# A second phase in which outputs are copied one tile later, two products share a PSUM buffer, and ACT takes one more chunk of the high part

## The chip, the cores and the metric

One core of a Trainium2 chip runs the program. The metric is the device time of one execution in microseconds (us), as the median of several runs. PE is the matrix engine (TensorE), DVE the vector engine, ACT the scalar engine, POOL is GpSimd, and SP only issues transfers (DMAs). PSUM is the memory that PE writes its products to; ACT and DVE read it, POOL and DMAs don't.

## The reference

```python
X = np.fft.rfft(x, axis=1)                    # 8 x 3072 x 256, in time
Y = X @ (w_r + 1j * w_i) + (b_r + 1j * b_i)   # then shrunk by 0.01
x = np.fft.irfft(shrink(Y), axis=1).reshape(24576, 256)
c, slot_out = soft_mixture(x, phi, w1, w2)    # 24576 x 32 and 32 x 256
x = c @ slot_out
h = x @ w_in                                  # 24576 x 1024
e = np.exp(h - h.max(-1, keepdims=True))
sm = e / (e.sum(-1, keepdims=True) + 1e-9)
solu = h * sm
mu, var = solu.mean(-1), solu.var(-1)         # kept as columns
ln = (solu - mu) / np.sqrt(var + 1e-6) * g_ln
out = ln @ w_out                              # 24576 x 256
```

The layers up to `c` are the program's first phase. In the second, `h` is computed as `c` times the small matrix `slot_out @ w_in`, and the rest of the last layer follows tile by tile.

## The kernel before, in words

The second phase (`phase2`, from line 840) is a loop over 192 tiles of 128 tokens, NI tiles in groups of four (NG = 48). Nothing schedules it but the order in which the loop writes its calls: each engine takes its own instructions in that order, and semaphores make it wait for other engines. One pass i of the loop (line 1170) works on several tiles at once, each at another stage:

- `hmat(i + 3)`: PE makes the rows of h (negated) in a PSUM buffer `hps` of two banks, one of three.
- `rowmax(i + 2)`: DVE takes the row minimum (L990) into the group's small tile `st`.
- `umul(i + 1)`: DVE multiplies `hps` by `e` into `u` and sums each row (L1005).
- `blocks(i + 1)`: DVE transposes u in blocks of 32 into `tb` (L1021), and SP issues four DMAs (L1025) that put the blocks in place in `t2`, one of three buffers. The profile calls this tile `t`.
- `store(i - 4)` and `late_c`: SP issues a group's output store (L1133), or loads `ct` for later tiles.
- `outp(i - 4)`: ACT copies the finished product from PSUM to `osb`, with the row's factor as its scale (L1122). The four copies of a group fill one `osb` buffer.
- `vari(i)`: ACT sums the squares of u's distance from its mean (`sq`, L1081).
- `uhi(i - 1)`: the high part of the transposed tile, rounded to the matrix engine's fast format; of eight chunks of 128 columns ACT makes the first HA = 5 (L1061), POOL the other three (L1062).
- `ulo(i - 1, 0)` and `ulo(i - 1, 1)`: POOL subtracts the high part from the tile, in two pieces (`ul`, L1071).
- `rstd(i)`, between those two pieces: in the last pass of each group POOL computes the factor of all four tiles, five operations on 4 columns (L1104 to L1108), the last a power of -1/2 into `st`. The last group does so for each tile.
- `expo(i + 2)`: ACT takes the exponential (`e`, L997).
- `prod(i - 2)`: PE multiplies the high and low parts by the two parts of the output weights, 24 matmuls into the PSUM buffer `po2` (`po` in the profile), one of two. A product waits for the copy of the tile two before it, which had its buffer.

On ACT the order of a pass is thus: `osb` of tile i-4, `sq` of i, `uh` of i-1, `e` of i+2. The last two tiles of all are transposed on PE (`direct`) instead of by DVE and DMA.

Of the kernel before, what the change touches and what calls it, by code (L numbers as in the profile page):

```python
# [8 lines left out]
F32 = mybir.dt.float32  # L9
# [5 lines left out]
ALU = mybir.AluOpType  # L15
# [20 lines left out]
def kernel(  # L36
# [24 lines left out]
    PE, ACT, DVE, POOL, SP = nc.tensor, nc.scalar, nc.vector, nc.gpsimd, nc.sync  # L61
    B, N, D = x.shape
# [5 lines left out]
    DFF = 1024  # L68
    NI = T // 128
# [18 lines left out]
    def mm(out, lhsT, rhs, start=True, stop=True):  # L88
        PE.matmul(out=out, lhsT=lhsT, rhs=rhs, start=start, stop=stop)  # L89
# [749 lines left out]
    def phase2(p2: ExitStack, pw: ExitStack):  # L839
# [24 lines left out]
        ps = pt.tile([128, 2, 32], F32, name="pslt", tag="pt")  # L864
# [81 lines left out]
        def right(name, bufs, **k):  # L946
            return p2.enter_context(tc.tile_pool(name=name, bufs=bufs, side="right", **k))
# [7 lines left out]
        po_p = right("po_p", 2, space=PSUM)  # L955
        NG = NI // 4
        ctt, hps, et, ut, uht, stt, osb, pot = {}, {}, {}, {}, {}, {}, {}, {}
# [13 lines left out]
        def hmat(i):  # L971
            if i >= NI:
                return
            j, k = divmod(i, 4)
            ps = ph_p.tile([128, DFF], F32, name="hps", tag="hps")
            for fh in range(2):
                mm(ps[:, 512 * fh:512 * fh + 512], ctt[j][:, 128 * k:128 * k + 128], (gstn if direct(i) else gst)[:, 512 * fh:512 * fh + 512])
            hps[i] = ps
# [7 lines left out]
        def rowmax(i):  # L986
            if i >= NI:
                return
            st, k = stats(i)
            DVE.tensor_reduce(out=st[:, 0, k:k + 1], in_=hps[i], op=ALU.min, axis=AX.X)  # L990
# [9 lines left out]
        def umul(i):  # L1000
            if i >= NI:
                return
            st, k = stats(i)
            u = u_p.tile([128, DFF], F32, name="u", tag="u")
            DVE.scalar_tensor_tensor(out=u, in0=hps.pop(i), scalar=1.0, in1=et.pop(i), op0=ALU.mult, op1=ALU.mult, accum_out=st[:, 2, k:k + 1])  # L1005
            ut[i] = u
# [10 lines left out]
        def blocks(i):  # L1017
            if i >= NI or direct(i):
                return
            t = u_p.tile([128, DFF], F32, name="tb", tag="tb", bufs=3)  # L1020
            DVE.transpose(out=t, in_=ut[i])  # L1021
            t2 = u_p.tile([128, 4, 256], F32, name="t2", tag="t2", bufs=3)
            for a in range(4):
                z = slice(32 * a, 32 * a + 32)
                SP.dma_start(out=t2[:, a, :], in_=t[z].rearrange("i (b x) -> i b x", b=4))  # L1025
            t2t[i] = t2

        def trans(i):
            if i >= NI or not direct(i):
                return  # L1030
            ps = ph_p.tile([128, 8, 128], F32, name="pu", tag="hps")
            for c in range(8):
                tp(ps[:, c, :], ut[i][:, 128 * c:128 * c + 128])
            ut[i, 0] = ps
# [7 lines left out]
        def direct_parts(i):  # L1042
            if i >= NI or not direct(i):
                return
            uh, ul = parts(i)
            ps = ut.pop((i, 0))
            for n in range(2):
                z = slice(4 * n, 4 * n + 4)
                ACT.activation(out=uh[:, z, :], in_=ps[:, z, :], func=AF.Copy)
                DVE.tensor_tensor(out=ul[:, z, :], in0=ps[:, z, :], in1=uh[:, z, :].bitcast(F32), op=ALU.subtract)  # L1050


        HA = 5

        def uhi(i):
            if i < 0 or direct(i):
                return
            uh, ul = parts(i)
            v = t2t[i].rearrange("p a (c j) -> p c a j", c=8)
            w = uh.rearrange("p c (a j) -> p c a j", a=4)  # L1060
            ACT.activation(out=w[:, 0:HA], in_=v[:, 0:HA], func=AF.Copy)  # L1061
            POOL.tensor_copy(out=w[:, HA:8], in_=v[:, HA:8])  # L1062

# [12 lines left out]
        def vari(i):  # L1076
            if i >= NI:
                return
            st, k = stats(i)
            sq = e_p.tile([128, DFF], F32, name="sq", tag="sq", bufs=1)  # L1080
            ACT.activation(out=sq, in_=ut.pop(i), func=AF.Square, bias=st[:, 2, k:k + 1], scale=-float(DFF), accum_out=st[:, 3, k:k + 1])  # L1081

        def prod(i):
            if i < 0 or i >= NI:
                return
            uh, ul = uht.pop(i)
            ps = po_p.tile([128, D], F32, name="po2", tag="po2")
            for f in range(8):
                mm(ps, uh[:, f, :], gw[:, f, 0, :], f == 0, False)
                mm(ps, uh[:, f, :], gw[:, f, 1, :], False, False)  # L1090
            for f in range(8):
                mm(ps, ul[:, f, :], gw[:, f, 0, :], False, f == 7)
            pot[i] = ps


        def rstd(i):
            if i >= NI:
                return
            j, k = divmod(i, 4)
            if j < NG - 1 and k < 3:  # L1100
                return
            st = stt[j]
            k = slice(0, 4) if k == 3 and j < NG - 1 else slice(k, k + 1)
            POOL.tensor_scalar(out=st[:, 1, k], in0=st[:, 1, k], scalar1=1e-9, scalar2=None, op0=ALU.add)  # L1104
            POOL.tensor_tensor(out=st[:, 1, k], in0=st[:, 1, k], in1=st[:, 1, k], op=ALU.mult)
            POOL.tensor_scalar(out=st[:, 1, k], in0=st[:, 1, k], scalar1=1e-6 * float(DFF) ** 3, scalar2=None, op0=ALU.mult)
            POOL.tensor_tensor(out=st[:, 3, k], in0=st[:, 3, k], in1=st[:, 1, k], op=ALU.add)
            POOL.tensor_tensor(out=st[:, 4, k], in0=st[:, 3, k], in1=mhalf[:, k], op=ALU.pow)  # L1108

# [2 lines left out]
        def outp(i):  # L1112
            if i < 0:
                return
            j, k = divmod(i, 4)
            b, r = divmod(j, 6)
            h, ah = divmod(r, 2)
            v = out.rearrange("(b h lm a) d -> b h lm a d", b=B, h=3, a=8)[b, h, :, 4 * ah:4 * ah + 4, :]
            if k == 0:
                osb[0] = o_p.tile([128, 4, D], F32, name="osb", tag="osb")  # L1120
            o = osb[0]
            ACT.activation(out=o[:, k], in_=pot.pop(i), func=AF.Copy, scale=stt[j][:, 4, k:k + 1])  # L1122
            if j == NG - 1:

                SP.dma_start(out=v[:, k, :], in_=o[:, k, :])
            elif k == 3:
                o_todo[i + 2] = (v, o)


        def store(i):  # L1130
            if i in o_todo:
                v, os2 = o_todo.pop(i)
                SP.dma_start(out=v, in_=os2)  # L1133
# [4 lines left out]
        def last_c(i):  # L1138
            d = [c_dram[B - 1, k].rearrange("h s x -> (h s) x") for k in range(2)]
            if i == 20:  # L1140
                cl[0] = o_p.tile([96, 1024], F32R, name="cl", tag="cl", bufs=1)
                cl[1] = o_p.tile([96, 1024], F32R, name="cl_h", tag="cl_h", bufs=1)
                SP.dma_start(out=cl[0].bitcast(F32), in_=d[0])
            elif i in (24, 26, 28, 30):
                z = slice(128 * (i - 24), 128 * (i - 24) + 256)
                POOL.tensor_copy(out=cl[1][:, z], in_=cl[0][:, z].bitcast(F32))
                POOL.tensor_tensor(out=cl[0][:, z], in0=cl[0][:, z].bitcast(F32), in1=cl[1][:, z].bitcast(F32), op=ALU.subtract)
            elif i == 33:
                SP.dma_start(out=d[0], in_=cl[1].bitcast(F32))
                SP.dma_start(out=d[1], in_=cl[0].bitcast(F32))  # L1150
# [3 lines left out]
        def late_c(i):  # L1154
            if i in c_todo:
                load_c(*c_todo.pop(i))
# [10 lines left out]
        expo(1)  # L1167
        umul(0)
        blocks(0)
        for i in range(NI + 4):  # L1170
            j, k = divmod(i, 4)
            hmat(i + 3)
            trans(i)
            rowmax(i + 2)
            umul(i + 1)
            blocks(i + 1)
            store(i - 4)
            late_c(i)
            last_c(i)
            outp(i - 4)  # L1180
            vari(i)
            direct_parts(i)
            if i <= NI:
                uhi(i - 1)
                ulo(i - 1, 0)
            rstd(i)
            if i <= NI:
                ulo(i - 1, 1)
            expo(i + 2)
            if i == 40:  # L1190
                gst_order()
            if k == 1:
                pieces(j + 2)
            prod(i - 2)
# [142 lines left out]
```

## Time and profile before

| | before |
|---|---|
| median of 3 runs | 1433.39 us (1429.41 to 1434.09) |
| profiled execution, its own time | 1435.42 us |
| its span, first to last instruction | 1433.6 us |
| mean granted TensorE clock, share of full speed | 0.962 |
| second phase, from its first row minimum | 654.95 us to the end |
| output copies, each 128x256 | 192 |

The page of the profile gives for each engine how long it was busy. What sets the time is read from the idle time: before each instruction the profile has the time that its engine stood idle, and what ended it (written `[2.63 <-POOL st L1108]` in a timeline). An instruction's length in the profile can reach into that of the next one on the same engine, so how much time a step takes is read from start to start.

### The profile page before, as it was taken

The numbers are of one execution on the slowest core, as the hardware profiler recorded it, in microseconds if no ns is written. First come the engines' busy times: TensorE is split into PE (matmuls) and PEld (weight loads), VectorE is DVE, ScalarE is ACT, GpSimd is POOL, SyncE is SP. The second block draws the span as 40 slices with busy tenths as digits, with TensorE's granted clock in tenths as the row PEclk, the third lists the DMA queues.
The fourth block names the chain that finished last, engine by engine and source line by source line (L and its number), as shares of the span: only waits on it lengthen the run. The fifth ranks groups of instructions, "written<-read, shape, count | busy, mean of one in ns | idle before, by whom it ended". The sixth has DMA issues, their size and how long they took to land.

```text
span 1433.6 us, 30947 instructions
## 1 busy us (share of the span) xinstructions
PE 1290.5 (90%) x10784; PEld 1155.4 (81%) x10784; DVE 1207.4 (84%) x1691; ACT 1018.1 (71%) x2005; POOL 1016.0 (71%) x1096
## 2 busy tenths in 40 slices
PE   6999999999999998886998888889888888899897
PEld 3888888888888887654887888888878888888787
DVE  6787989897979797757998888989988889899884
ACT  5567665657575754335887788888878887888785
POOL 5556565757474733313889898888888888888886
PEclk8999999999999999998999999999999999999999
DMA  8965373637373643394677777777777777777664
GB/s 267 292 185 173 115 210 100 210 90 213 98 210 101 194 155 98 121 348 98 162 202 176 205 182 178 192 178 177 187 182 190 177 189 186 181 176 193 178 166 118
DMA packets 190746, 252.70 MB, mean 176 GB/s; under 512 B 21504, under 2 KB 155392, under 8 KB 190592
## 3 DMA queue, kind: packets, MB, share of 16 engines
q1 hardware_dynamic: 190256, 249.57, 63.8%
q8 instruction: 85, 1.39, 0.4%
q10 hardware_dynamic: 336, 1.18, 0.2%
q14 instruction: 69, 0.57, 0.1%
HBM read 91.94 MB, written 59.11 MB: 105 GB/s over the span
## 4 chain that ended last, share of the span: by engine, by line
PE 31%; ACT 16%; DVE 14%; POOL 12%; DMA 10%; issue 10%; SPq 6%; ACTq 0%; POOLq 0%; DVEq 0%
DMA t<-tb 8%; PE pb L89 6%; POOL ul L1071 6%; ACT sq L1081 6%; SPq L1025 5%; PE pm L89 5%; PE po L89 5%; PE s L89 4%; ACT e L997 4%; PE xps L89 4%; ACT uh L1061 3%; PE pa L89 3%; PE sps L92 2%; DVE tb L1021 2%; POOL st L1108 2%
## 5 line engine op out<-in xcount | busy, mean ns | idle before, releaser
L1071 POOL TENSOR_TENSOR ul<-t,uh 128x512 fp32r<-128x512 f32 x380 | 485.4, 1294 | 57.6 <-ACT uh L1061 55.7
L89 PEld LDWEIGHTS po<-gw,uh 128*128 128x128 f32 x3072 | 406.3, 198 | 120.9 <-ACT osb L1122 108.4
L89 PE MATMUL po<-gw,uh 128*128 128x256 f32 x3072 | 420.8, 292 | 88.3 <-ACT osb L1122 88.2
L1005 DVE SCALAR_TENSOR_TENSOR u<-hps,e 128x1024 f32<-128x1024 f32 x192 | 232.7, 1212 | 78.2 <-ACT e L997 78.2
L343 POOL TENSOR_TENSOR s<-yb,s 128x512 f32<-128x512 f32 x95 | 132.2, 1392 | 218.2 <-DVE s L342 190.3
L1021 DVE STREAM_TRANSPOSE tb<-u 128x1024 f32<-128x1024 f32 x190 | 236.6, 1246 | 6.6
L990 DVE TENSOR_REDUCE st<-hps 128x1 f32<-128x1024 f32 x192 | 227.6, 1186 | 2.1 <-PE hps L89 1.8
L1081 ACT ACTIVATE sq<-u,st 128x1024 f32<-128x1024 f32 x192 | 221.8, 1155 | 0.2 <-DVE u L1005 0.2
L89 PE MATMUL po<-gw,ul 128*128 128x256 f32 x1536 | 219.4, 286 | 1.9 <-POOL ul L1071 1.9
L997 ACT ACTIVATE e<-hps,st 128x1024 f32<-128x1024 f32 x192 | 213.6, 1113 | 4.1 <-DVE st L990 4.1
L89 PEld LDWEIGHTS po<-gw,ul 128*128 128x128 f32 x1536 | 202.0, 195 | 2.5 <-POOL ul L1071 2.5
L1122 ACT ACTIVATE osb<-po,st 128x256 f32<-128x256 f32 x192 | 91.3, 475 | 132.4 <-POOL st L1108 126.1
L235 POOL TENSOR_TENSOR x<-xc,x 96x512 fp32r<-96x512 f32 x120 | 162.4, 1362 | 31.4 <-ACT x L234 29.5
L1061 ACT ACTIVATE uh<-t 128x640 fp32r<-128x640 f32 x190 | 140.1, 737 | 11.8 <-DMA t<-tb 10.7
L1062 POOL CAST uh<-t 128x384 fp32r<-128x384 f32 x190 | 96.6, 508 | 47.9 <-DMA t<-tb 45.4
L89 PE MATMUL hps<-gst,ct 128*128 128x512 f32 x380 | 119.9, 398 | 9.6 <-DVE u L1005 8.2
L261 ACT ACTIVATE asb<-s 96x512 f32<-96x512 f32 x112 | 66.6, 595 | 72.3 <-PE s L89 72.2
L89 PE MATMUL s<-x,df_h 96*96 96x512 f32 x240 | 104.8, 439 | 11.6 <-ACT x L234 4.5
L89 PEld LDWEIGHTS xps<-d_sb,apt 128*128 128x128 f32 x768 | 99.3, 194 | 13.8 <-issue 2.9
L89 PE MATMUL xps<-d_sb,apt 128*128 128x128 f32 x768 | 105.7, 281 | 1.9 <-DMA apt<-ad 1.1
L234 ACT ACTIVATE x<-xc 96x512 fp32r<-96x512 f32 x120 | 75.2, 626 | 14.1 <-DMA xc<-in_x_dram 14.0
L297 DVE TENSOR_TENSOR xsum<-xps,xi 128x256 f32<-128x256 f32 x96 | 39.7, 413 | 52.3 <-ACT xh L296 49.6
(202 smaller groups left out, 2248.1 us busy)
## 6 DMA issues: line engine op xcount, KB each, us to landing
t<-tb SPq DMA_DIRECT2D x760, 128.0 KB, 2.9
apt<-ad SPq DMA_DIRECT2D x96, 256.0 KB, 4.1
out_dram<-osb SPq DMA_DIRECT2D x47, 512.0 KB, 3.6
xc<-in_x_dram SPq DMA_DIRECT2D x56, 384.0 KB, 4.0
ad<-asb SPq DMA_DIRECT2D x56, 384.0 KB, 3.4
ct<-c_dram SPq DMA_DIRECT2D x96, 128.0 KB, 3.2
wt<-in_moe_w_dram SPq DMA_DIRECT2D x21, 512.0 KB, 9.0
ws<-in_moe_w_dram SPq DMA_DIRECT2D x22, 256.0 KB, 5.5
```

Source lines behind the costliest of these rows:

```text
L89: PE.matmul(out=out, lhsT=lhsT, rhs=rhs, start=start, stop=stop)
L235: POOL.tensor_tensor(out=lo, in0=t, in1=hi.bitcast(F32), op=ALU.subtract)
L343: (DVE if (b, t) == (B - 1, NT - 1) else POOL).tensor_tensor(out=s, in0=yb, in1=s, op=ALU.subtract)
L990: DVE.tensor_reduce(out=st[:, 0, k:k + 1], in_=hps[i], op=ALU.min, axis=AX.X)
L997: ACT.activation(out=e, in_=hps[i], func=AF.Exp, bias=st[:, 0, k:k + 1], scale=-1.0, accum_out=st[:, 1, k:k + 1])
L1005: DVE.scalar_tensor_tensor(out=u, in0=hps.pop(i), scalar=1.0, in1=et.pop(i), op0=ALU.mult, op1=ALU.mult, accum_out=st[:, 2, k:k + 1])
L1021: DVE.transpose(out=t, in_=ut[i])
L1061: ACT.activation(out=w[:, 0:HA], in_=v[:, 0:HA], func=AF.Copy)
L1062: POOL.tensor_copy(out=w[:, HA:8], in_=v[:, HA:8])
L1071: POOL.tensor_tensor(out=ul[:, z, :].rearrange("p c (a j) -> p c a j", a=4), in0=v, in1=w.bitcast(F32), op=ALU.subtract)
L1081: ACT.activation(out=sq, in_=ut.pop(i), func=AF.Square, bias=st[:, 2, k:k + 1], scale=-float(DFF), accum_out=st[:, 3, k:k + 1])
L1122: ACT.activation(out=o[:, k], in_=pot.pop(i), func=AF.Copy, scale=stt[j][:, 4, k:k + 1])
```

## The change

Four things change, all in the second phase. The copy and the store of a finished product come one pass later (tile i - 5 in pass i), and the loop has one pass more. A PSUM buffer `po2` holds the products of two tiles, an even one and the odd one after it, so that the same two banks hold four products. The factor takes four operations: the first one adds 1e-9 and multiplies by the root of the constant, which the squaring after it then contains. ACT makes six of the eight chunks of the high part, POOL two.

```diff
-        HA = 5
+        HA = 6
...
-            ps = po_p.tile([128, D], F32, name="po2", tag="po2")
+            if i % 2 == 0:
+                pot[i // 2, 0] = po_p.tile([128, 2, D], F32, name="po2", tag="po2")
+            ps = pot[i // 2, 0][:, i % 2, :]
...
-            POOL.tensor_scalar(out=st[:, 1, k], in0=st[:, 1, k], scalar1=1e-9, scalar2=None, op0=ALU.add)
+            POOL.tensor_scalar(out=st[:, 1, k], in0=st[:, 1, k], scalar1=1e-9, scalar2=(1e-6 * float(DFF) ** 3) ** 0.5, op0=ALU.add, op1=ALU.mult)
             POOL.tensor_tensor(out=st[:, 1, k], in0=st[:, 1, k], in1=st[:, 1, k], op=ALU.mult)
-            POOL.tensor_scalar(out=st[:, 1, k], in0=st[:, 1, k], scalar1=1e-6 * float(DFF) ** 3, scalar2=None, op0=ALU.mult)
             POOL.tensor_tensor(out=st[:, 3, k], in0=st[:, 3, k], in1=st[:, 1, k], op=ALU.add)
             POOL.tensor_tensor(out=st[:, 4, k], in0=st[:, 3, k], in1=mhalf[:, k], op=ALU.pow)
...
-        for i in range(NI + 4):
+        for i in range(NI + 5):
...
-            store(i - 4)
+            store(i - 5)
             late_c(i)
             last_c(i)
-            outp(i - 4)
+            outp(i - 5)
```

Two tables of the order of instructions show what this moves. The first is ACT in the middle of the second phase, before; `po_` and a number is a product's PSUM buffer as it was allocated, and behind `waits` stand the engines whose semaphores the instruction waits for.

```order
L1081 ACTIVATE sq,st<-u,st 128x1024 [waits DVE_49,Activation_49]
L1061 ACTIVATE uh<-t_11180 128x640 [waits DMAHW6_49,DMAHW7_49,DMAHW5_49,DMAHW4_49]
L997 ACTIVATE e,st<-hps,st 128x1024 [waits DVE_49]
L1122 ACTIVATE osb<-po_11250,st 128x256 [waits PE_49]
L1081 ACTIVATE sq,st<-u,st 128x1024 [waits DVE_49,Activation_49]
L1061 ACTIVATE uh<-t_11229 128x640 [waits DMAHW2_49,DMAHW3_49,DMAHW1_49,DMAHW0_49]
L997 ACTIVATE e,st<-hps,st 128x1024 [waits DVE_49]
L1122 ACTIVATE osb<-po_11300,st 128x256 [waits PE_49]
```

The same engine and place with the change:

```order
L1123 ACTIVATE osb<-po_11165,st 128x256
L1081 ACTIVATE sq,st<-u,st 128x1024 [waits DVE_49,Activation_49]
L1061 ACTIVATE uh<-t_11250 128x768 [waits DMAHW6_49,DMAHW7_49,DMAHW5_49,DMAHW4_49]
L997 ACTIVATE e,st<-hps,st 128x1024 [waits DVE_49]
L1123 ACTIVATE osb<-po_11266,st 128x256 [waits PE_49]
L1081 ACTIVATE sq,st<-u,st 128x1024 [waits DVE_49,Activation_49]
L1061 ACTIVATE uh<-t_11299 128x768 [waits DMAHW2_49,DMAHW1_49,DMAHW3_49,DMAHW0_49,Pool_49]
L997 ACTIVATE e,st<-hps,st 128x1024 [waits DVE_49]
L1123 ACTIVATE osb<-po_11266,st 128x256
```

The order within a pass stays, `osb` is that of a tile earlier (next to the `uh` of a given transfer), two copies read one buffer, and of the two only the first, the even tile's, waits for PE: the wait covers the odd tile's product too.

On POOL, at the end of the phase's first group, the difference is this (- before, + with the change):

```order
-L1104 TENSOR_SCALAR st<-st 128x4
-L1105 TENSOR_TENSOR st<-st 128x4 [waits Pool_49]
-L1106 TENSOR_SCALAR st<-st 128x4 [waits Pool_49]
-L1107 TENSOR_TENSOR st<-st 128x4 [waits Pool_49]
-L1108 TENSOR_TENSOR st<-st,mhalf 128x4 [waits Pool_49]
+L1106 TENSOR_SCALAR st<-st 128x4
+L1107 TENSOR_TENSOR st<-st 128x4 [waits Pool_49]
+L1108 TENSOR_TENSOR st<-st 128x4 [waits Pool_49]
+L1109 TENSOR_TENSOR st<-st,mhalf 128x4 [waits Pool_49]
 L1071 TENSOR_TENSOR ul<-t_9080,uh 128x512
```

The factor stays where it was, ahead of the second piece of the low part, with one operation less.

## Rows read from the trace of the kernel before

**Rows 1.** Page: busy us; window: length, PE, PEld, DVE, ACT, POOL, PEclk, DMA share, GB/s.

```profile
PE 1290.5 (90%) x10784; PEld 1155.4 (81%) x10784; DVE 1207.4 (84%) x1691; ACT 1018.1 (71%) x2005; POOL 1016.0 (71%) x1096
...
900.00:1000.00 100.00, 88.42 (x651) 84.20 (x652) 88.72 (x102) 81.99 (x152) 88.17 (x109) 0.95 0.72 181
```

**Rows 2.** Waits from 650 us on: waiter, releaser, us in total, times, longest us.

```profile
ACT osb L1122 <- POOL st L1108: 126.1, 47, 3.7
...
PE po L89 <- ACT osb L1122: 88.2, 47, 3.4
DVE u L1005 <- ACT e L997: 78.2, 51, 2.8
...
ACT uh L1061 <- DMA t<-tb: 10.7, 12, 2.4
```

**Rows 3.** Timeline of ACT: start us, us, instruction, [idle before <-releaser].

```profile
670.26 0.74 ACT L1061 ACTIVATE uh<-t 128x640 fp32r<-128x640 f32 x1 [2.35 <-DMA t<-tb]
...
677.70 0.47 ACT L1122 ACTIVATE osb<-po,st 128x256 f32<-128x256 f32 x1 [2.75 <-POOL st L1108]
...
917.25 0.47 ACT L1122 ACTIVATE osb<-po,st 128x256 f32<-128x256 f32 x1 [2.63 <-POOL st L1108]
...
920.48 0.47 ACT L1122 ACTIVATE osb<-po,st 128x256 f32<-128x256 f32 x1
...
923.69 0.48 ACT L1122 ACTIVATE osb<-po,st 128x256 f32<-128x256 f32 x1
...
932.85 0.47 ACT L1122 ACTIVATE osb<-po,st 128x256 f32<-128x256 f32 x1 [2.62 <-POOL st L1108]
...
1407.57 0.47 ACT L1122 ACTIVATE osb<-po,st 128x256 f32<-128x256 f32 x1 [2.62 <-POOL st L1108]
```

**Rows 4.** Timeline of POOL around one factor.

```profile
913.61 1.30 POOL L1071 TENSOR_TENSOR ul<-t,uh 128x512 fp32r<-128x512 f32 x1 [0.24 <-ACT uh L1061]
914.99 0.24 POOL L1104 TENSOR_SCALAR st<-st 128x4 f32<-128x4 f32 x1
...
915.60 0.23 POOL L1106 TENSOR_SCALAR st<-st 128x4 f32<-128x4 f32 x1
...
917.19 1.29 POOL L1071 TENSOR_TENSOR ul<-t,uh 128x512 fp32r<-128x512 f32 x1
...
922.78 2.55 POOL L1071 TENSOR_TENSOR ul<-t,uh 128x512 fp32r<-128x512 f32 x2 [0.22 <-ACT uh L1061]
```

**Rows 5.** Timeline of DVE.

```profile
672.12 1.23 DVE L1005 SCALAR_TENSOR_TENSOR u<-hps,e 128x1024 f32<-128x1024 f32 x1 [0.40 <-ACT e L997]
...
904.98 1.23 DVE L1005 SCALAR_TENSOR_TENSOR u<-hps,e 128x1024 f32<-128x1024 f32 x1 [1.38 <-ACT e L997]
...
913.32 1.25 DVE L1021 STREAM_TRANSPOSE tb<-u 128x1024 f32<-128x1024 f32 x1
...
926.59 1.18 DVE L990 TENSOR_REDUCE st<-hps 128x1 f32<-128x1024 f32 x1
...
930.12 1.18 DVE L990 TENSOR_REDUCE st<-hps 128x1 f32<-128x1024 f32 x1
```

**Rows 6.** Timeline of PE: two products without a wait.

```profile
921.16 2.04 PE L89 MATMUL po<-gw,uh 128*128 128x256 f32 x16
...
924.43 2.04 PE L89 MATMUL po<-gw,uh 128*128 128x256 f32 x16
```

**Rows 7.** SP's issue of one tile's transfers, and the landing times of tile t.

```profile
914.70 2.49 SPq L1025 DMA_DIRECT2D t<-tb  x4
...
DMA to landing us min/median/max: 2.5/2.9/5.5
```

**Rows 8.** Groups by line: count | busy us, mean ns | idle us before.

```profile
L1061 ACT ACTIVATE uh<-t 128x640 fp32r<-128x640 f32 x190 | 140.1, 737 | 11.8 <-DMA t<-tb 10.7 <-POOL ul L1071 0.9
...
L1062 POOL CAST uh<-t 128x384 fp32r<-128x384 f32 x190 | 96.6, 508 | 47.9 <-DMA t<-tb 45.4 <-PE po L89 1.5 <-PE hps L89 0.9
...
L1146 POOL CAST cl_h<-cl 96x256 fp32r<-96x256 f32 x4 | 1.6, 400 | 0.0
```

## The prediction

> **What bounds the kernel now.** Busy shares first [rows 1]: over the whole program PE is busy 90%, DVE 84%, ACT and POOL 71%; inside the second phase, which the change touches, four engines lie close together (PE 88, DVE 89, ACT 82, POOL 88 of 100 us). No engine is full, so something periodic holds them all. The waits say what [rows 2]. ACT's copy of a finished product into the output buffer (`osb`, L1122) waits for POOL's factor (L1108) 126.1 us in 47 waits; there are 48 groups of four tiles, so that is one wait of some 2.7 us per group. PE (88.2 us, 47 waits) and DVE (78.2 us, 51 waits) wait for ACT in turn. Transfers end few waits: 10.7 us before ACT's `uh`, in 12 tiles.
>
> The timeline of ACT shows the cycle [rows 3]: the copy at 917.25 waited 2.63 us, the next ones start 3.2 us apart without a wait (920.48, 923.69), and at 932.85 the next group begins with 2.62 us again. From the first such wait (677.70) to the last (1407.57) lie 46 groups, 729.9 us, so a group takes 15.87 us.
>
> POOL shows why the factor is late [rows 4]: it begins the four-tile factor between the two `ul` pieces of the group's third tile. The pieces start at 913.61 and 917.19, 3.58 us apart, where two pieces in a row take 2.55 together; the factor's five operations fill the difference. ACT wants the factor in the very next pass and gets it 2.63 us late.
>
> Now the floor of each engine where it doesn't wait. DVE: two row minima (926.59, 930.12) lie 3.53 us apart, 14.1 per four tiles, and its wait for `e` once a group is 1.38 us (904.98) [rows 5]. ACT: 3.21 us from copy to copy, 12.8 per four [rows 3]. PE: 3.27 us from product to product (921.16, 924.43), 13.1 per four [rows 6]. POOL: 88.17 us busy in 100, so 14.0 in 15.87 [rows 1]. DVE has the highest floor, and of what it loses now 47 x 1.38 = 64.9 us is the periodic wait; the other 13.3 of its 78.2 us come from transfers that land late in some groups.
>
> **The change part by part.**
>
> *The copy one tile later.* ACT copies tile i-5 instead of i-4 in pass i, so the first copy of a group comes one ACT pass later: 3.21 us, or 3.53 once DVE sets the pace, against 2.63 us of lateness. The wait goes, with 0.6 to 0.9 us to spare before the next part is counted. ACT then has nothing periodic left to wait for, `e` comes in time, and DVE's 64.9 us go with it. This is the whole gain.
>
> *Two tiles to a PSUM buffer.* Without it PE would now wait for the later copies. The product of an even tile waits for the copy of tile i-3, which stands at the head of the same ACT pass as its present one (i-2); the odd tile finds its half free. In return the copy of an even tile waits for the product of the odd tile after it, as the order of ACT shows, and the odd copy has no wait. That product is issued on PE in pass i+3, the copy on ACT in pass i+5. With DVE setting the pace, count from the start of its pass i+2: `u` ends after some 2.3 us and frees the buffer that PE needs first, so with its 3.27 us PE is done after 5.6 to 8 us (8, if it lost 2.4 to late pieces); ACT reaches the copy after `e` of pass i+4, two passes (7.06) and some 3.7 us later, at 10.8. So at least 2.8 us are spare, an estimate from the pitches above, and I cost this at nothing in the loop. At the very end it costs: the copy of the last even tile has to wait for the last product, so two copies of 0.47 us [rows 3] follow that product instead of one, +0.5 us. The bounds are 0 (the store hides it) and 1 us.
>
> The Trainium skill ("PSUM — Partial Sum Buffer", section "PSUM bank collisions raise a hardware error") says that TensorE may not write a bank while ScalarE reads another place of that same bank, so that two tiles in one bank must be guarded together. By it the even copy could in no case start before the odd product has ended; the order of ACT says the same, and no trace of before shows the case, since each product has its own buffer. Whether that guard costs time is the rival on the slow side, below.
>
> *Four small operations.* POOL drops one of five per group: two of them start 0.61 us apart (914.99, 915.60), so 0.31 us [rows 4]. The first operation takes a second scalar: no trace shows it at this shape; below by 0 (it stays at the 0.24 us of 914.99), above by another 0.24. I take 0: it has four elements to a row, and its time is start, not data. It is off the path once the copy comes later; it adds 0.1 to 0.3 us to the margin.
>
> *Six chunks on ACT.* ACT's `uh` grows from 640 to 768 columns a row, POOL's from 384 down to 256 [rows 8]. ACT: from its 0.47 us copy of 256 columns [rows 3] and 737 ns for 640 [rows 8], 0.70 ns a column gives 0.09 us; in proportion to 640 it is 0.15; I take 0.12, near the middle, as two rows can't tell start from data. POOL: in proportion, 508 falls to 339 ns; a 256-column cast of another tile took 400; so 0.11 to 0.17 us are saved. ACT's floor becomes 4 x 3.33 = 13.3 us per four tiles, POOL's 14.0 - 4 x 0.11 - 0.31 = 13.2. Both stay below DVE's 14.1, which covers the extra ACT work; were that cover gone, it would cost 190 x 0.12 = 23 us.
>
> *What is late next.* With DVE steady the transferred tile (`t`) is the nearest. From the end of a transposition to the `u` of three tiles later DVE itself needs 2 x 3.53 and a row minimum of 1.18, 8.2 us [rows 5]. On the other side: the transposition at 913.32 ends at 914.57, its four transfers start at 914.70 and take SP 2.49 us [rows 7], the last starts about 1.9 us after the first and lands a median 2.9 us later: 4.9 us after the end. From ACT's `uh` to the `u` that follows (670.26 to 672.12 [rows 3, 5]) are 1.9 us, plus 0.12. That is 6.9 of 8.2 us; a tile may land about 1.3 us later than usual before DVE waits. The longest landing took 5.5 us for the 2.9, so some will. I keep the 13.3 us that they cost now and add 3, since the DMA share of 0.72 [rows 1] rises in the ratio of the group times to about 0.79. The ends are 3 us for all of it (no group hit any more, as ACT loses no time elsewhere) and 37 us (the first rival).
>
> *Sum.* The profiled execution took 1435.4 us. 1435.4 - 64.9 + 3.0 + 0.5 = 1374.0. It stood 2.0 us above the median of the three runs, 1433.4, so against that median I expect **1372 us**. A group would take about 14.5 us.
>
> **Rivals.**
>
> *Late transfers take over (1393 us).* For: SP has one queue, and an output store or the loads of `ct` delay the next transfer; the path above has only 1.3 us to spare, and POOL's factor still delays the release of a `t2` buffer once a group. Against: four tiles in a row already run at DVE's pace between two waits, with the same transfers. If each group loses 0.8 us to them, 46 x 0.8 = 37 us stay instead of 16.3: 1372 + 21 = 1393. A factor that still comes 1.3 us late in each group would give the same: 13.3 + 1.3 - 14.1 = 0.5 us more a group, 1395.
>
> *No change (1430 to 1437 us).* The change doesn't do what it says if POOL falls a whole pass behind as well: ACT then finds the same 2.6 us one pass later. For: POOL is as busy as DVE. Against: in ordinary tiles POOL itself waits for ACT (0.22 us before the pieces at 922.78 [rows 4]), so it catches up, and its work gets shorter.
>
> *Slower: the even copy waits for PE (1468 us).* Two tiles share a buffer, so 96 copies wait for a product that comes 3.3 us after their own. If PE has lost its 2.8 us of lead, ACT stands w us at each. ACT needs 13.3 + 2w for four tiles; it decides from w = 0.4 (14.1), and the time passes that of before from w = 1.3 (15.87). With half a product, w = 1.65, a group takes 16.6 us: 46 x 0.73 = 34 us over before's 1433.4, with the tail 1468. For: PE is late by the factor's delay in one tile of four, and catches up only 0.26 us a tile. Against: the 88.2 us that PE now waits for `osb` [rows 2] come from the late factor, and go with it.
>
> **How the numbers follow.** Forecast 0.62, late transfers 0.28, no change 0.04, slower 0.06. The range: the forecast's own lower end, 1372 - 13 = 1359, so 1360, up to the first rival's value and a little over, 1398. A measurement of this kernel tells some 0.3% from no change (4.3 us): faster 0.90, same 0.04, slower 0.06.
>
> **What would show it.** Right: before `osb` hardly any idle time ends with POOL's factor; DVE's idle time before `u` falls from 78 to some 16 us; DVE is busy over 95% of the second phase; ACT's `uh` takes 0.83 to 0.89 us and now shows waits for `t`; POOL's factor is four operations. Wrong: `osb` waits for PE or still for POOL, or DVE's idle time stays above 45 us with `uh` waiting for transfers in most groups.

## The result, and the profile after

The changed kernel takes 1370.8 us (median of 4 runs, 1370.69 to 1372.79); beside it the kernel before took 1431.8 us (median of 4, 1429.41 to 1434.09). The ratio is 0.9577, with a 95% interval of 0.9557 to 0.9598: 4.2% faster. The forecast was 1372.

The profiled execution has a span of 1368.9 us, 64.7 us less than the 1433.6 of before. Its page and two windows of the changed kernel (length, then busy time of PE, PEld, DVE, ACT and POOL, then PEclk, DMA share, GB/s) answer to [rows 1]:

```profile
span 1368.9 us, 30896 instructions
...
PE 1272.0 (93%) x10784; PEld 1129.9 (83%) x10784; DVE 1203.2 (88%) x1691; ACT 1040.3 (76%) x2005; POOL 976.7 (71%) x1045
...
700.00:1300.00 600.00, 563.96 (x4290) 528.40 (x4289) 579.90 (x661) 556.20 (x991) 545.96 (x670) 1.00 0.79 201
...
900.00:1000.00 100.00, 93.03 (x707) 86.95 (x706) 96.57 (x110) 92.64 (x168) 89.15 (x110) 1.00 0.79 200
```

The same 600 us of the kernel before:

```profile
700.00:1300.00 600.00, 529.54 (x3932) 503.40 (x3932) 532.30 (x605) 490.81 (x906) 530.63 (x653) 0.96 0.73 185
```

DVE is now busy 96.7% of the window, where it had 88.7%; no other engine is over 94%. The busy time of the whole program hardly moved (DVE 1207.4 to 1203.2 us, PE 1290.5 to 1272.0): the gain is idle time that is gone. SP issued 605 of the transfers into `t` in this window before and 659 now, four to a tile. So a group of four took 600 / 605 x 16 = 15.87 us and takes 14.57 now, as these rows of line L1025 in that window show, before first, then after:

```profile
L1025 SPq DMA_DIRECT2D t<-tb x605: 542/602/1796, 699.9 to 1299.6; - x152
```

```profile
L1025 SPq DMA_DIRECT2D t<-tb x659: 542/603/1859, 699.6 to 1299.9; - x165
```

The waits from 650 us on, of the changed kernel (waiter, releaser, us, times, longest), answer to [rows 2]:

```profile
POOL uh L1062 <- DMA t<-tb: 52.2, 20, 38.0
ACT uh L1061 <- DMA t<-tb: 47.9, 58, 2.4
PEld po L89 <- ACT osb L1123: 37.2, 44, 1.8
...
PE po L89 <- POOL ul L1071: 22.0, 44, 1.4
PE po L89 <- ACT osb L1123: 19.2, 28, 1.4
DVE u L1005 <- ACT e L997: 16.3, 31, 1.5
...
ACT osb L1123 <- PE po L89: 6.0, 2, 4.9
```

The row that led the list of before, `osb` for POOL's factor with 126.1 us in 47 waits, is not there any more. DVE's wait for `e` fell from 78.2 to 16.3 us: 61.9 of the 64.7 us of the span. What is left is irregular: ACT waits for a transferred tile in 58 tiles, against 12 before (10.7 us then, 47.9 now). POOL's 52.2 us hold one wait of 38.0 ahead of the first tile.

The timeline of ACT in the changed kernel shows what takes the place of [rows 3]:

```profile
902.73 0.85 ACT L1061 ACTIVATE uh<-t 128x768 fp32r<-128x768 f32 x1 [1.14 <-DMA t<-tb]
...
904.57 0.47 ACT L1123 ACTIVATE osb<-po,st 128x256 f32<-128x256 f32 x1
...
907.88 0.47 ACT L1123 ACTIVATE osb<-po,st 128x256 f32<-128x256 f32 x1
...
911.19 0.48 ACT L1123 ACTIVATE osb<-po,st 128x256 f32<-128x256 f32 x1
```

Three copies in a row wait for nothing; they start 3.31 us apart, which is ACT's own floor for a tile when nothing holds it. A late transfer (1.14 us) is all that ACT loses here, and of that 0.64 us reaches DVE, whose next row minima are 3.53 us apart again:

```profile
904.70 1.23 DVE L1005 SCALAR_TENSOR_TENSOR u<-hps,e 128x1024 f32<-128x1024 f32 x1 [0.64 <-ACT e L997]
...
907.14 1.19 DVE L990 TENSOR_REDUCE st<-hps 128x1 f32<-128x1024 f32 x1
...
910.67 1.19 DVE L990 TENSOR_REDUCE st<-hps 128x1 f32<-128x1024 f32 x1
```

POOL's timeline around a factor, which answers to [rows 4]: the pieces of `ul` start 3.17 us apart (906.97 and 910.14), 0.41 less than before.

```profile
906.97 1.27 POOL L1071 TENSOR_TENSOR ul<-t,uh 128x512 fp32r<-128x512 f32 x1 [0.43 <-ACT uh L1061]
908.33 0.19 POOL L1106 TENSOR_SCALAR st<-st 128x4 f32<-128x4 f32 x1
...
910.14 1.28 POOL L1071 TENSOR_TENSOR ul<-t,uh 128x512 fp32r<-128x512 f32 x1
```

The groups of the two halves of the high part answer to [rows 8] (count, busy us, mean ns, idle us before):

```profile
L1061 ACT ACTIVATE uh<-t 128x768 fp32r<-128x768 f32 x190 | 160.8, 846 | 51.4 <-DMA t<-tb 47.9
L1062 POOL CAST uh<-t 128x256 fp32r<-128x256 f32 x190 | 76.0, 400 | 54.6 <-DMA t<-tb 52.2
```

### The profile page after: what moved, and what is told of

It is laid out like the page before. It is cut to its first block, busy times and chain, and to the rows that moved or that the text cites. A ratio compares the mean times of both kernels' runs of the same rounds, so it can differ in the third digit from the quotient of the medians.

```text
span 1368.9 us, 30896 instructions
## 1 busy us (share of the span) xinstructions
PE 1272.0 (93%) x10784; PEld 1129.9 (83%) x10784; DVE 1203.2 (88%) x1691; ACT 1040.3 (76%) x2005; POOL 976.7 (71%) x1045
## 4 chain that ended last, share of the span: by engine, by line
PE 29%; DVE 18%; DMA 17%; issue 10%; POOL 9%; SPq 9%; ACT 6%; POOLq 0%; DVEq 0%; ACTq 0%
DMA t<-tb 11%; SPq L1025 8%; PE pb L89 7%; POOL ul L1071 6%; PE pm L89 5%; PE s L89 4%; DVE tb L1021 4%; PE xps L89 4%; PE po L89 3%; DVE u L1005 3%; PE pa L89 3%; DMA xc<-in_x_dram 3%; PE sps L92 2%; ACT uh L1061 2%; ACT e L997 1%
## 5 line engine op out<-in xcount | busy, mean ns | idle before, releaser
L89 PEld LDWEIGHTS po<-gw,uh 128*128 128x128 f32 x3072 | 386.0, 189 | 49.7 <-ACT osb L1123 37.2
L89 PE MATMUL po<-gw,uh 128*128 128x256 f32 x3072 | 398.7, 282 | 19.9 <-ACT osb L1123 19.2
L89 PE MATMUL po<-gw,ul 128*128 128x256 f32 x1536 | 228.0, 285 | 22.6 <-POOL ul L1071 22.0
L1005 DVE SCALAR_TENSOR_TENSOR u<-hps,e 128x1024 f32<-128x1024 f32 x192 | 232.5, 1211 | 17.0 <-ACT e L997 16.3
L89 PEld LDWEIGHTS po<-gw,ul 128*128 128x128 f32 x1536 | 198.7, 188 | 34.2 <-POOL ul L1071 33.9
L1061 ACT ACTIVATE uh<-t 128x768 fp32r<-128x768 f32 x190 | 160.8, 846 | 51.4 <-DMA t<-tb 47.9
L1062 POOL CAST uh<-t 128x256 fp32r<-128x256 f32 x190 | 76.0, 400 | 54.6 <-DMA t<-tb 52.2
L89 PEld LDWEIGHTS xps<-d_sb,apt 128*128 128x128 f32 x768 | 99.3, 194 | 13.3 <-issue 2.9
L234 ACT ACTIVATE x<-xc 96x512 fp32r<-96x512 f32 x120 | 75.2, 626 | 12.7 <-DMA xc<-in_x_dram 12.5
```

## The experiments

The theory is that one ring of waits held the phase once a group: POOL's factor, ACT's copy, ACT's own work of the passes that follow up to `uh`, POOL's first piece of `ul`, and the next factor. These lines of the kernel before, ACT's first and POOL's below, close it:

```profile
928.38 0.75 ACT L1061 ACTIVATE uh<-t 128x640 fp32r<-128x640 f32 x1
```

```profile
929.21 1.30 POOL L1071 TENSOR_TENSOR ul<-t,uh 128x512 fp32r<-128x512 f32 x1 [0.22 <-ACT uh L1061]
930.59 0.23 POOL L1104 TENSOR_SCALAR st<-st 128x4 f32<-128x4 f32 x1
...
931.78 1.04 POOL L1108 TENSOR_TENSOR st<-st,mhalf 128x4 f32<-128x4 f32 x1
```

From the copy at 917.25 [rows 3] ACT works without a wait until this `uh` ends at 929.13; POOL's piece waits for it, the factor follows, and the copy at 932.85 waits for the factor: 15.60 us around, in a group without a late transfer. DVE and the transfers are not links of this ring; DVE is held by it, in its wait for `e`. The copy one pass later opens it, and the shared buffer keeps PE from closing another. Rivals: the delay alone does it; the shared buffer alone does it, since it takes away PE's waits; the smaller factor does it. None of the kernels leaves out a part of the computation. Ratios are against the kernel before, run on the same chip, with 95% intervals.

| kernel | copy | products to a buffer | factor ops | ACT chunks | us | ratio |
|---|---|---|---|---|---|---|
| before | i-4 | 1 | 5 | 5 | 1432 to 1435 | 1 |
| small parts alone | i-4 | 1 | 4 | 6 | 1428.35 | 0.9971 (0.9956 to 0.9986) |
| no delay | i-4 | 2 | 4 | 6 | 1430.38 | 0.9985 (0.9967 to 1.0002) |
| delay alone | i-5 | 1 | 5 | 5 | 1423.43 | 0.9937 (0.9907 to 0.9966) |
| delay and pair | i-5 | 2 | 5 | 5 | 1376.23 | 0.9605 (0.9574 to 0.9635) |
| five operations | i-5 | 2 | 5 | 6 | 1378.10 | 0.9605 (0.9587 to 0.9623) |
| five chunks | i-5 | 2 | 4 | 5 | 1369.22 | 0.9553 (0.9534 to 0.9572) |
| the change | i-5 | 2 | 4 | 6 | 1370.80 | 0.9577 (0.9557 to 0.9598) |
| delay of two | i-6 | 2 | 4 | 6 | 1450.67 | 1.0114 (1.0090 to 1.0139) |

**The delay alone.** Against before:

```diff
-        for i in range(NI + 4):
+        for i in range(NI + 5):
-            store(i - 4)
+            store(i - 5)
-            outp(i - 4)
+            outp(i - 5)
```

> The kernel before with nothing changed but the later copy and store (tile i-5 in pass i, one pass more); every product keeps its own PSUM buffer, five operations for the factor, five chunks on ACT. Theory (the wait for the factor is what the change removes, and the shared buffer is needed so that PE doesn't wait for the later copies): from a copy at the head of an ACT pass to the end of e one pass later lie 0.5 (copy) + 3.3 (product) + 0.6 (hmat) + 1.2 (row minimum) + 1.1 (e) = 6.7 us, and DVE's pace leaves 7.06, so any late piece shows: 1380 to 1410 us, PE waiting for osb before most products. Rival (the later copy alone is the whole gain): 1366 to 1376 us.

Measured 1423.43 us, a gain of 0.6%: the theory's kind (PE waits for the copy), but more of it than the theory's range allowed. `osb` waits for the factor once, 1.2 us. PE waits instead, and DVE waits for PE. The waits from 650 us on:

```profile
PEld po L89 <- ACT osb L1122: 129.7, 127, 3.3
...
PE po L89 <- ACT osb L1122: 79.5, 89, 3.1
...
DVE st L990 <- PE hps L89: 54.7, 61, 3.0
```

One turn of this second ring in the timelines of PE and DVE, and the windows of the same stretch (columns as above):

```profile
901.84 3.44 PE L89 MATMUL po<-gw,uh 128*128 128x256 f32 x16 [1.82 <-ACT osb L1122]
```

```profile
906.98 1.23 DVE L990 TENSOR_REDUCE st<-hps 128x1 f32<-128x1024 f32 x1 [2.65 <-PE hps L89]
```

```profile
900.00:901.80 1.80, 0.02 (x1) 0.00 (x0) 1.80 (x2) 1.80 (x5) 1.53 (x3) 1.00 0.75 172
901.80:905.10 3.30, 3.26 (x17) 3.26 (x18) 2.49 (x4) 3.30 (x7) 3.05 (x4) 0.58 0.68 149
```

PE stands 1.82 us, and then its granted clock is 0.58 over the next 3.3 us, near the lower of its two levels (1.2 of 2.4 GHz): 16 matmuls take 3.44 us where [rows 6] have 2.04. The wait of 1.82 us is so followed by another 1.4, and DVE loses 2.65. That is not every turn: by the trace's clock records the lower level was granted for 17.1 us in all between 700 and 1300 us, against 54.6 us in the kernel before. The mean stays at 0.99:

```profile
700.00:1300.00 600.00, 537.94 (x4000) 492.45 (x3999) 544.38 (x614) 508.78 (x925) 538.03 (x665) 0.99 0.75 189
```

So the waits themselves hold this kernel, and the clock adds to a few of them.

**Delay and pair.** The same with the shared buffer (`po_p.tile([128, 2, D], ...)`, as in the change):

> The change without its two small parts: later copy and shared PSUM buffer, but five operations for the factor and five chunks on ACT. Theory: POOL's floor stays at 14.0 us per four tiles against DVE's 14.1, so nearly the whole gain is there, 1371 to 1385 us, with POOL's pieces later than in the changed kernel. Rival (the small parts carry a share of their own): 1385 us or more.

Measured 1376.23 us, within the theory. From 700 to 1300 us DVE is 577 of 600 us busy, at a clock of 1.00. So these two parts together bring 3.95%. The later copy alone brings 0.6%; the shared buffer was not run quite alone, but together with the small parts (next run) it brings nothing that these parts don't bring without it.

**No delay.** Against the changed kernel:

```diff
-        for i in range(NI + 5):
+        for i in range(NI + 4):
-            store(i - 5)
+            store(i - 4)
-            outp(i - 5)
+            outp(i - 4)
```

> The change without the later copy: shared PSUM buffer, four operations, six chunks on ACT, copy of tile i-4 in pass i. Theory: ACT still waits for POOL's factor, some 2.4 us a group, and the copy of an even tile now waits for the odd tile's product as well, since the 2.8 us to spare shrink by a pass of 3.5: 1430 to 1460 us. Rival (the small parts bring the gain): under 1415 us.

Measured 1430.38 us, the lower end of the theory. Waits from 650 us on:

```profile
ACT osb L1123 <- POOL st L1109: 105.4, 47, 2.4
POOL ul L1071 <- ACT uh L1061: 95.1, 170, 0.9
...
DVE u L1005 <- ACT e L997: 75.2, 49, 2.3
PE po L89 <- POOL ul L1071: 72.5, 55, 1.9
```

PE waits for no copy any more, where [rows 2] had 88.2 us of it, and nothing is gained by that. So its wait for the copy was no part of what held the group. It waits for POOL's `ul` instead. Two of the other rows are the first ring: POOL's factor holds ACT, and ACT's `uh` holds POOL; the third is DVE, which ACT's `e` holds (75.2 us, as the 78.2 of before). The second half of the theory is small here: copies waited for a product 9.4 us in 11 waits, against 4.7 us in 2 before.

**Small parts alone.** Before, with four operations and six chunks:

```diff
-        HA = 5
+        HA = 6
-            POOL.tensor_scalar(out=st[:, 1, k], in0=st[:, 1, k], scalar1=1e-9, scalar2=None, op0=ALU.add)
+            POOL.tensor_scalar(out=st[:, 1, k], in0=st[:, 1, k], scalar1=1e-9, scalar2=(1e-6 * float(DFF) ** 3) ** 0.5, op0=ALU.add, op1=ALU.mult)
-            POOL.tensor_scalar(out=st[:, 1, k], in0=st[:, 1, k], scalar1=1e-6 * float(DFF) ** 3, scalar2=None, op0=ALU.mult)
```

> The kernel before with the two small parts alone: four operations for the factor, six chunks on ACT; own PSUM buffers, copy of tile i-4. Theory: the factor comes 0.31 us earlier, ACT's four passes take 0.5 us longer, so a group is as long as before: 1425 to 1440 us. Rival (the small parts bring the gain): under 1415 us.

Measured 1428.35 us, as the theory has it. `osb` waits for the factor 105.7 us in 47 waits (126.1 before), and little of that reaches the end: the factor takes some 0.4 us less (the pieces around it start 3.19 us apart, 3.58 before), but four `uh` of 845 ns take 0.43 more than four of 737, and both stand in the ring.

**Five chunks, and five operations.** The changed kernel with one small part undone each. Five chunks:

```diff
-        HA = 6
+        HA = 5
```

> The changed kernel with five chunks on ACT again (later copy, shared buffer, four operations). The kernel with neither small part took 1376.2, the changed one 1370.8. Theory (POOL near its floor is what the small parts relieve, and the chunk relieves it by 0.11 us a tile, 0.44 a group, the dropped operation by 0.31 a group): the chunk is worth the larger half, so 1373 to 1375 us. Rival (only the dropped operation counts): 1370 to 1371.5 us.

Five operations, the three lines of the factor as before:

> The changed kernel with five operations for the factor again (later copy, shared buffer, six chunks on ACT). Theory: the dropped operation is worth the smaller half of the 5.4 us, so 1372 to 1374 us. Rival (only the dropped operation counts): 1375 to 1377 us.

Both lie on the rival's side, each about 1 us outside its range. With five chunks the time is 1369.22 us, no slower than with six: the sixth chunk does nothing that these runs can tell. With five operations it is 1378.10. Delay and pair against five chunks differ by the dropped operation alone: 0.9605 to 0.9553, 0.5% or some 7 us, with intervals that just stay apart (each kernel beside before on its own chip). Five operations against the change: 0.28%, some 4 us, with intervals that overlap. So the dropped operation is worth some 4 to 7 us, once the ring is open. The waits of the kernel with five operations show where; these are SP's own, from 650 us on, and below them the same two of the changed kernel:

```profile
SPq L1025 <- DVE tb L1021: 66.8, 82, 13.3
SPq L1025 <- POOL uh L1062: 49.4, 61, 1.7
```

```profile
SPq L1025 <- DVE tb L1021: 75.6, 105, 13.0
SPq L1025 <- POOL uh L1062: 29.6, 45, 1.7
```

SP may not fill a `t2` buffer before POOL has read it. The rows name POOL's cast, but by the program's order the last to read the buffer is the second piece of `ul` just ahead of that cast, the piece that stands behind the factor. Worked out from the starts and ends in the traces between 700 and 1300 us: with five operations this piece ended after both the transposition and SP's previous issue in 47 tiles and held the transfer for 32.2 us in all; in the changed kernel in 40 tiles for 18.5 us, with five chunks in 38 for 18.9, with the delay and the pair in 51 for 35.1. DVE's wait for `e` is 21.9 us with five operations instead of 16.3. How busy POOL is doesn't tell the fast kernels from the slow: with five chunks it works 564 of 600 us, with five operations 551. The chunk takes as much of POOL's time in a group (0.43 us) as the operation (0.41), but not all in one place ahead of a release.

**A fourth buffer for the transferred tile.** If that release were all, one more buffer should take it away. The changed kernel with

```diff
-            t2 = u_p.tile([128, 4, 256], F32, name="t2", tag="t2", bufs=3)
+            t2 = u_p.tile([128, 4, 256], F32, name="t2", tag="t2", bufs=4)
```

> The changed kernel with a fourth t2 buffer, so that SP no longer waits for POOL's pieces of the tile three before. Theory (DVE's remaining 16.3 us of waiting come from transfers that land late, and some of those because SP's issue waits for POOL to free a buffer, 42 us in all): the issue waits for POOL go, DVE's wait before u falls below 10 us, 1360 to 1368 us. Rival (the late landings come from SP's own order and the transfers themselves, and POOL's waits are covered): DVE's wait stays at 14 to 18 us, 1368 to 1373 us.

Measured 1367.49 us, ratio 0.9536 (0.9518 to 0.9555). By the same working the release holds no transfer any more (18.5 us before), but ACT's wait for the transfer falls only from 47.9 to 45.0, and DVE's to 14.3. The time lies where the theory put it, the wait where the rival did. So the rest of the late tiles are late for another reason than the buffer. What the trace still has is SP's own order: in 64 of 164 tiles SP was issuing something else when the tile was ready, 58.2 us in all. With five chunks as well:

> The changed kernel with five chunks on ACT and a fourth t2 buffer. Each alone took 1369.2 and 1367.5 us. Theory (both give the transfers some time, and what is left is SP's order): 1365 to 1369 us. Rival (POOL's release is what is left): under 1364 us.

1369.24 us, 0.9539 (0.9513 to 0.9565): at the upper end of the theory, and no different from either.

**The delay of two.** The changed kernel with `NI + 6`, `store(i - 6)` and `outp(i - 6)`:

> The changed kernel with the copy yet another tile later (tile i-6 in pass i, two passes more), the shared buffer as it is. Theory (the shared buffer pays for one pass of delay only): an even tile's product now waits for a copy at the head of the next ACT pass, as every product did with the later copy in own buffers (1423 us), here every other one: 1385 to 1420 us, with PE waiting for osb and DVE for hps. Rival (two shared buffers are room enough): 1368 to 1374 us.

Measured 1450.67 us, slower than before by 1.1%, and beyond the theory's range. Waits from 650 us on, and one turn in DVE's timeline:

```profile
PEld po L89 <- ACT osb L1123: 130.9, 81, 4.3
PE po L89 <- ACT osb L1123: 99.7, 63, 3.9
...
DVE st L990 <- PE hps L89: 70.2, 47, 3.8
```

```profile
900.11 1.23 DVE L990 TENSOR_REDUCE st<-hps 128x1 f32<-128x1024 f32 x1 [3.00 <-PE hps L89]
```

It is the second ring again. The order of the program tells when it closes: PE issues the product of tile n in pass n+2. Before, it needs the copy of n-2, which ACT makes in that same pass; in the changed kernel an even tile needs that of n-3, again in pass n+2. In the delay alone and in the delay of two, the copy stands in pass n+3, one pass after the product that needs it. Why two passes cost more than the delay alone, where every product waits and not every other, is not shown: PE's waits are longer (99.7 us in 63 against 79.5 in 89), and the clock from 700 to 1300 us is 0.96 against 0.99.

**The store on ACT's queue.** To free SP's queue for the transfers, from the five chunks:

```diff
-                SP.dma_start(out=v, in_=os2)
+                ACT.dma_start(out=v, in_=os2)
```

> The changed kernel with five chunks on ACT and the output stores issued by ACT instead of SP. Theory (the transfers that land late, on which DVE's last 14 to 16 us of waiting hang, are late because SP issues one thing after another: 2.5 us for a tile's four, 0.6 for a store, 1.9 for the loads of ct): the store's 0.6 us a group leave SP, and ACT has room for them, so DVE's wait falls to 8 to 12 us and the time to 1362 to 1368 us. Rival (the late ones come from POOL's release of buffers and from the transfers themselves): no change against five chunks alone, 1367 to 1372 us, or slower if ACT's issue delays e.

Theory and rival were both wrong: 1409.92 us, 0.9834 (0.9807 to 0.9861), 40 us slower than the five chunks. The waits from 650 us on, and ACT's timeline at a store:

```profile
ACT uh L1061 <- DMA t<-tb: 104.3, 56, 4.2
...
DVE u L1005 <- ACT e L997: 52.9, 44, 3.0
```

```profile
908.46 0.37 ACTq L1134 DMA_DIRECT2D out_dram<-osb  x1
...
914.05 0.74 ACT L1061 ACTIVATE uh<-t 128x640 fp32r<-128x640 f32 x1 [2.28 <-DMA t<-tb]
```

The issue takes ACT 0.37 us; it isn't that. ACT's wait for transfers grows from 60.6 to 104.3 us. Worked out from the landing times in the trace between 700 and 1290 us: of tiles whose first transfer is issued in the 1.8 us ahead of a store, the last piece lands a median 7.3 us after the transposition's end (37 tiles). With the store on SP, the tiles issued just before it take 5.2 (39 tiles), those just behind it 5.5 (40). That fits a store which runs beside the transfers from a second queue and takes their share, where on one queue it follows them. But ACT also issues it at another moment, among the issues of a tile's transfers and not behind them; these runs don't tell the queue from the moment, and what exactly the store holds up was not settled. With the fourth buffer too:

> The changed kernel with all three: five chunks on ACT, a fourth t2 buffer, stores issued by ACT. Theory (SP's order is the larger cause of the late landings): under 1364 us, DVE's wait below 10 us. Rival (neither is): 1366 to 1370 us.

1399.53 us, 0.9759 (0.9732 to 0.9786), both wrong for the same reason: ACT waits 98.7 us for transfers. Beside it on the same chip, five chunks and the fourth buffer with the store on SP took 1369.24, so there the store's move costs 30 us.

**The changed kernel again**, beside the last three:

> The changed kernel as it is, on the same chip as the three beside it, so that they can be compared with it directly: 1368 to 1374 us by every theory.

1373.69 us, 0.9577 (0.9552 to 0.9601), the first ratio once more. The fourth buffer and the five chunks lie 0.2 to 0.4% below, with intervals that meet it; that either beats the change is not shown.

## Why the prediction was right

*What bounds the kernel.* Right. The first ring was read from [rows 2 to 4]. The kernel without the delay shows that PE's waits were no part of it: with their 88.2 us taken away, the time stays at 0.9985. And it differs from the changed kernel by the delay alone, 1430.38 against 1370.80 us.

*The copy one tile later: -64.9 us.* The mechanism was right. DVE's wait fell by 61.9 us and the forecast's rest of 16.3 us is what the row says. That the rest agrees to the tenth is luck: the 13.3 us that the prediction put down to late transfers are a difference, and in DVE's timeline of before only some 8 of them stand in groups with a late transfer, the others in the first and last tiles and in three groups in which POOL had other work. The margin held: with the delay and the pair alone `osb` waits for the factor only once (0.6 us). Yet the time is then 1376, not 1372, and the reason is not this wait but the release of `t2`: it held transfers for 35.1 us, where the kernel with five chunks, which differs by the dropped operation alone, has 18.9.

*Two tiles to a buffer.* "Without it PE would now wait for the later copies" was right, and the price of that was not worked out: 47 us between the delay alone and the delay with the pair. With the buffer, `osb` waits for PE only at the end of the program (6.0 us in 2 waits): the 2.8 us of lead that the prediction estimated were enough in every pass, and the slow rival fell. The rule that the prediction names, of the Trainium skill ("PSUM — Partial Sum Buffer", section "PSUM bank collisions raise a hardware error"), that a bank which ScalarE reads may not be written meanwhile, asks for the order that the program keeps here. Its price in the loop is not to be seen in these waits: before, with a buffer for each product, `osb` also waited for PE at the end, 4.7 us in 2 waits. No run shows what would happen without that order. At the end two copies follow the last product, in 0.84 us instead of 0.47: +0.4 against +0.5.

*Four small operations: nothing on the path.* This is the term that was wrong: put at nothing, it measured some 4 to 7 us. The prediction saw that POOL's factor "delays the release of a `t2` buffer once a group", but put it into a rival and not into the sum. The two-scalar operation costs less than its lower bound: 194 ns against 235 for the one it replaces, so the factor shrank by 0.41 us where 0.31 was counted.

*Six chunks.* ACT's 846 ns are 0.11 more than 737 (0.12 taken); POOL's cast took 400, the higher of the two values given. That DVE "covers the extra ACT work" is right within the noise: without that work, with five chunks, the kernel takes 1369.22 us, 1.6 less and with intervals that overlap, far from the 23 us that were the price without the cover.

*What is late next.* The tile in transfer, as said: ACT waits for it 47.9 us in 58 tiles at a DMA share of 0.79, as forecast, and a third of that reaches DVE. The path had less to spare than the 1.3 us that the prediction worked out: it takes the last piece to land 4.9 us after the transposition's end, and worked out from the traces between 700 and 1300 us that is a median 5.2 us before and 5.5 with the change. That the sum came out within 1.2 us owes something to two small errors against each other: the forecast has no gain from the dropped operation, and the delay with the pair fell short of it by as much.

## What to carry to other kernels

When a result waits for a late factor once a period, move its consumer later by about the lateness, and check in the same step, buffer by buffer, that the writer of the next result doesn't now ask for a buffer whose reader stands a pass behind it: the delay without the room gained 0.6%, with it 4%, and one pass too many lost 1%. The longest list of waits isn't the bound: 88 us of PE's waits could be taken away for nothing, since they only followed from the ring. Once the ring is open, small work counts again where it stands ahead of a release that another engine waits for: 0.4 us a group in the factor were worth some 4 to 7 us, and as much POOL time in the casts nothing that these runs can tell.

## What the runs showed of the hardware

- A wait of 1.82 us on PE was followed by 3.3 us at a granted clock of 0.58, in which 16 matmuls took 3.44 us instead of 2.04. In the changed kernel, where PE's own waits for copies and for `ul` last at most 1.4 us, the clock is 1.00 from 700 to 1300 us (0.96 before). The clock is not what made it faster: the delay alone has 0.99 in that stretch and gains 0.6%.
- On POOL, `tensor_scalar` on 128x4 with two scalars took 194 ns and with one 235 and 226, in 47 instructions of each.
- A 512 KB store per group issued from ACT, in 0.37 us each, goes by a queue of its own in the profile and made the kernel 40 us slower (30 with the fourth buffer). From SP's queue, behind a tile's transfers, the tiles beside the same store land a median 5.2 and 5.5 us after their transposition, as other tiles do.
